# A state-space convolution in blocks of 1024: the sums of the second block's spectrum products move from VectorE and TensorE to accumulating transfers, under a new instruction order

## The chip, the cores and the metric

The kernel runs on one core of one Trainium2 chip. The metric is the device time in microseconds (us) of one execution. A profile of one execution is at hand for the kernel before; it names the engines PE (TensorE: matmuls), DVE (VectorE), ACT (ScalarE), POOL (GpSimd) and SP (SyncE, which here only issues transfers).

## The reference, cut to what matters

Two branches over 2048 tokens of 512 channels are mixed by a gate. Branch A is a long convolution, whose kernel K comes from a state-space model; branch B is a small expert network for the two tokens with the highest scores.

```python
P = jnp.exp(logdA[:, :, None] * l[None, None, :])
K = jnp.einsum("dn,dnl,dn->dl", Cc, P, dB).real        # 512 x 2048
...
Yf = Uf * Kf                                           # spectra, zero-padded to 2 L
y = irfft(Yf)[..., :L] + u * Dskip                     # branch A
...
r = x @ w_r; idx = argsort(-r)[:, :2]                  # branch B: two tokens
y = (silu(x_sel @ w_gate) * (x_sel @ w_up)) @ w_down
...
return g * a + (1 - g) * b
```

## The kernel before

**Blocks.** The sequence is cut into two blocks of 1024 tokens, and K likewise into K0 and K1. The spectra of the blocks are X0 and X1. The first block's result needs X0 K0. The second block's needs X1 K0 + X0 K1, and the sum of these two spectrum products is what the change is about. The 512 channels are handled in two halves (`h` = 0, 1) of 256, the frequencies in two quadrants (`qd` = 0, 1).

**Stages.** The order of the program text is this; engines run ahead of each other as far as the data allow.

1. Loads, exponentials and sines (`exps1`, `exps2`, `trig`, `tab1`, `tab2`) that give tables for K, mostly on ACT and DVE; the routing of branch B (`routing`) beside it.
2. `forward`: the spectra of the input by matmuls (L881).
3. `kgen(h)`: K at chosen lags by matmuls (L899), then a selection by matmuls (L912 to L928). Its last step multiplies an 8x256 result of these by a stored one on DVE.
4. `kspec(h)`: the spectrum of K by matmuls (L954), with a carry through the identity in the first half (L946).
5. `products(h, qds, blks)`: the spectrum products on DVE. For each half, block and quadrant, one 128x4096 product (all four combinations of real and imaginary parts) is written to a tile `p`; for the second block (`blk` 1) a second 128x4096 product, of X0 and K1, to a tile `t`. The two are summed, then real and imaginary parts combined (`u(0) - u(3)`, `u(1) + u(2)`: two of 128x1024), then written back to X as sums and differences of even and odd parts.
6. `inverse(h)`: ACT first copies a part of the output into PSUM (the seeds), then matmuls (L1028, and L1016 for a few edge tokens) add the inverse transform, ACT or DVE scales the result into the tile U (L1036), and 16 transfers of 128 KB write the output.

**How the second block is summed.** For three of the four pairs (half, quadrant) DVE adds the two tiles in one 128x4096 sum. For the pair named in `ACC`, (1, 0), PE adds them: identity matmuls (L990) form sum and combination in PSUM, and ACT moves the two results back.

**Order and places.** Nothing is scheduled at run time. `ORDER` is a string with the order of all operations, `SECOND` says which of two engines runs an operation that has a choice (evictions, scalings, squares: `EV`, `SCL`, `SQ` in the new kernel), `PLACES` which place in a pool of buffers a short-lived tile gets. `Prog` derives the semaphore waits from what each operation reads and writes. Each engine executes its own list strictly in order. A tile's place is free again when the last reader of its former tile has run. `late()` clears the edge tile OHR on POOL (L861), and SP's load of c_oh waits for it; the 2 MB load of the inverse matrices (c_inv, to tile G) and a part of the reload of U stand behind it in SP's queue.

Of the kernel before, what the change touches and what calls it, by code (L numbers as in the profile page):

```python
# [241 lines left out]
MUL1 = [(16, 4, 24, 4, 1), (20, 0, 24, 4, 1), (28, 15, 24, 4, -1)]  # L242
# [11 lines left out]
ACC = ((1, 0),)  # L254
# [98 lines left out]
def small_mats():  # L353
# [15 lines left out]
POOLS = {"pqa": 2, "pqb": 2, "pqc": 4}  # L369
ORDER = (  # L370
    "01l00200k01501600500000u00100400700o00p00q00601j01g00t00w00v01001201h01d01901e01100900r01a00300s01701x00801v00d00g00h02701t00x01r01y01400y01300c00f00z"
    "00l02500b00i01800a02801c01s01w01p01q00n00e02302601u02101z05n02402002201b03w04002901f06i01o01n03x08d03y06h08f05m02a02j03v02k01i04102l08e01m02b06j02m03z"
    "02n02c02o00m03702p05302q02r04202d02s06k02t06l04302u03404b05402v02w04506m04405h02x04802y04902z04a04c03003804603103204p04d05503904q04f03304704g04e04i04j"
    "03c03503l03d04h05g04k05o04m04r06p03g04l04n04u06q05q03h04o06n04s03i04w06o04t05604v06w03k00j03p03o06v06y06x03m03j06r08r01k06s04y03a04z03605p05707003n06z"
    "05805b05006t05i05907107204x07307405a08i08q05r05c06u07607505108g08j08h07807705205k08s05j05z07a03q08k07905d07h07b08t05l03b08u03r05e07c05s06003s07e07f03t"
    "07g07i08l06107j07d06606508n08v06306708x08o08y05f08m08w06206806909l06a08p08z07l07k07n09009206409u09m07m07o07q07z07r09107p09409309509n07s09o09r09609p07w"
    "07u09t07t07x09q09s09z0970980800a006b06c09c0990a20a102e09a09b09d08a06d09v09w05u05t09e0a30a408909g06f09h0a60a509x09f0a70a809i0aa06e0a905v07v05w07y05x03e"
    "06g08308403f09y09k0ac0ab08109j0ad0ae0820ag08b0af08508808c03u0aq0ar0ay0860aj0as0at05y0az0ao0ap0au0ah0ai0al0ak0am0an0b00b10av0aw0ax0ch0b80b90bc0be0870bb"
    "0bi0bf02f0ba0bd0bh0ci0cj0bg0bk0c40c10bj02g0ck0bz0cl0bl0bn0bm0b50bw02h0bo0b20b60c00b30b40br0c30bx0c20by0bp0bs0bq0bt0b70ct0bu02i0c50c60c70c90e80e70e90c8"
    "0cm0cu0bv0cn0co0cr0cv0d30cs0ea0cy0cb0eg0ez0cp0d40cw0cx0cz0eb0eh0cq0d10em0ep0d00e60d50ec0d20d60f40ed0e50d70f00f50ee0f10f20f60eq0df0er0ca0cc0dg0ei0es0f9"  # L380
    "0ef0f30ce0cd0f70f80dh0dn0fw0d80fx0dc0db0d90fy0ej0cf0dl0g40da0ek0en0et0fa0cg0dp0dv0dd0eu0di0dj0dk0do0dy0fz0de0eo0fs0g00dz0e00dq0dm0ds0g10g50dr0ft0fb0fc"
    "0g20fu0fv0el0fd0fe0fg0gc0gp0ff0dw0gm0dx0gd0g60g30go0gn0ge0gq0gt0gr0dt0fh0fi0fk0fj0ey0gf0g90gx0gu0ev0gg0ga0gs0e40e30du0gb0e20ew0e10g70gi0gw0gh0ex0gv0gz"
    "0fl0gk0fm0fo0fn0gl0gy0h80h00fp0h40fq0h10fr0h20g80gj0h50h30h60h70hh0hg0hc0h90ha0hd0he0hi0hf0hb0hj"
)
SECOND = (
    "000000000000000000000000000000000000100000000000000000000000000010101000101010100000000100000000000000000000000000100010000000000000000000000001000101"
    "001110010100010010000010010010000100000000000000000000000000000000000000000000000000000000001010000010000000000001000000000000000000000000000000000000"
    "000000000101000000010100011010000010011010000000100010001000001000000000000000000000000000000000000000000000000000000000000000000000000000000000000000"
    "000000000000000000000000000000000000000000000000000000000000000000000000000000000000000000000000000000000000000000000000000000000000001000000000000000"
    "00000000000000010000001100100000"  # L390
)
PLACES = (
    "2004756176414666666067000110100264042421011602064766100101111004004220204264646600000004406600706142350206200227354163"
# [4 lines left out]
def bass_gated_mix__ssm_conv_s4__moe_arch_mod__prompt_kernel(nc, A_u, A_A_re, A_A_im, A_B_re, A_B_im, A_C_re, A_C_im, A_log_dt, A_Dskip,  # L398
# [22 lines left out]
    with ExitStack() as es:  # L421
# [8 lines left out]
        def B(name, off, nbytes, dt=BF):  # L430
            assert off + nbytes <= SBW and off % 2 == 0, (name, off, nbytes)
            return Buf(P, name, AR, "sb", int(off), int(nbytes), dt)
# [9 lines left out]
        def nel(ap):  # L442
            r = 1
            for s, c in ap.ap[1:]:
                r *= c
            return r
# [3 lines left out]
        def TT(o, a, b, op, rd, wr, cst=None, **k):  # L450
            return P.op(DVE, lambda h: h.tensor_tensor(out=o, in0=a, in1=b, op=op), rd, wr, cost=cst or tt_cost(o, a, b), **k)  # L451
# [12 lines left out]
        def EV(o, a, rd, wr, **k):  # L464
            n = nel(o)
            return P.op((ACT, DVE), (lambda h: h.activation(out=o, in_=a, func=ACTF.Copy), lambda h: h.tensor_copy(o, a)), rd, wr,  # L466
                        cost=(0.185 + n * 0.833e-3, 0.16 + n * (1.04e-3 if a.dtype == F32 else 0.52e-3)), **k)
        def AFF(o, a, c, d, rd, wr):
            return P.op((DVE, ACT), (lambda h: h.tensor_scalar(out=o, in0=a, scalar1=c, scalar2=d, op0=ALU.mult, op1=ALU.add), lambda h: h.activation(out=o, in_=a, func=ACTF.Copy, scale=c, bias=d)), rd, wr, cost=(0.18, 0.2))
# [53 lines left out]
        PQR = [[B("pqa", oTI[0], 8 * KB), B("pqb", oTI[0] + 8 * KB, 8 * KB)], [B("pqc", oI, 16 * KB)] * 2]  # L523
        def place(pool, region, off, nbytes, dt=BF, n=1):
            def home(u):
                a = AR[:, (off + u * nbytes) // 2:(off + (u + 1) * nbytes) // 2]
                return (a if dt == BF else a.bitcast(dt)), 0
            return Life(P, pool, n, home, region, pool)
        OHR = B("ohr", oR, len(ERT) * 256)
        class Mem:  # L530
            def __init__(self, name):
                self.name, self.w, self.r, self.all, self.alias = name, {}, {}, [], []
# [80 lines left out]
        def pair(a, b):  # L613
            return bass.AP(a.tensor, a.offset, [a.ap[0], [b.offset - a.offset, 2]] + list(a.ap[1:]))
# [39 lines left out]
        def tab1(h, ts):  # L654
            tr = TP[h][1]
            e = lambda *ss: [(tr, ("e", s)) for s in ss]
            for o, a, b, n, d in MUL1:
                src = [a + i * d for i in range(n)]
                assert all(T1[o + i] == T1[x] + T1[b] for i, x in enumerate(src))
                v = lambda s0, st: tr(0, 128, 4 * s0, (128, 64), (st, n), (1, 4))  # L660
                TT(v(o, 4), v(a, 4 * d), v(b, 0), ALU.mult, e(b, *src), e(*range(o, o + n)))
# [32 lines left out]
        def tab2(h, ts):  # L694
# [11 lines left out]
            TT(pair(q2(0), q2(1)), pair(sq(eb, 0), sq(di, 0)), pair(sq(eb, 0), sq(di, 0)), MUL, ed, [(qa, 0), (qa, 1)])  # L706
# [254 lines left out]
        def products(h, qds, blks):  # L961
# [11 lines left out]
            tmp = lambda k: place("pq%s" % ("ab"[k] if h == 0 else "c"), PQR[h][k], (oTI[0] + 8 * k * KB, oI)[h], 8 * W, n=2)  # L973
            qk = lambda b, *ks: [(b, k) for k in ks]
            for blk in blks:
                p = tmp(0)
                TT(o2(p), x2(blk), k2(0), MUL, kx(blk) + kk(0, 0) + kk(0, 1), qk(p, 0, 1, 2, 3))
                if blk == 1:
                    t = tmp(1)
                    TT(o2(t), x2(0), k2(1), MUL, kx(0) + kk(1, 0) + kk(1, 1), qk(t, 0, 1, 2, 3))  # L980
# [14 lines left out]
                else:  # L995
                    if blk == 1:
                        TT(vall(p), vall(p), vall(t), ADD, qk(t, 0, 1, 2, 3), qk(p, 0, 1, 2, 3))
# [119 lines left out]
```

## Time and profile before

| What | Value |
|---|---|
| Median of 3 runs (lowest, highest) | 153.64 us (153.03, 154.14) |
| The profiled execution's own time | 153.67 us |
| Its span, first to last instruction | 151.9 us |
| Mean granted clock of TensorE | 0.988 |
| Busy: PE, DVE, ACT, POOL | 140.4, 140.1, 128.3, 6.7 us |
| 128x4096 products and sums on DVE | 15, mean 2282 ns |
| Identity matmuls that add the products (L990) | 16, 3.7 us busy |
| ACT's evictions of 128x1024 from PSUM | 34, mean 1021 ns |

A row of the groups has the line, the engine, the operation, what is written and read (partitions x elements), the count, then busy time and the mean of one in ns, then the idle time of the engine just ahead of them with what ended it. Many instructions of DVE have one line, 451, because a helper issues them; they are told apart by their shapes. In the chain of waits each row is a start, a length and the work that ran; "issue" is time in which an engine waited for nothing that the profile shows. In the slices, each digit stands for a fortieth of the span.

### The profile page before, as it was taken

How to read it: one execution, taken by the hardware profiler on the slowest of the kernel's cores; microseconds unless marked ns; L12 is line 12 of the kernel's file. 1: busy time of each engine (PE TensorE's matmuls, PEld its weight loads, DVE VectorE, ACT ScalarE, POOL GpSimd, SP SyncE). 2: the span in 40 equal slices, each digit the busy share in tenths (PEclk: the TensorE clock that was granted, in tenths of full speed). 3: DMA queues.
4: the chain of work that ended last, by engine and by line, in shares of the span. 5: the costliest groups of instructions: out<-in, count | busy, mean ns of one | idle time of the engine just before them, and what ended most of it. 6: DMA issues, size and time to landing. Idle time of an engine off the chain costs nothing.

```text
span 151.9 us, 3913 instructions
## 1 busy us (share of the span) xinstructions
PE 140.4 (92%) x1677; PEld 101.9 (67%) x1677; DVE 140.1 (92%) x201; ACT 128.3 (84%) x215; POOL 6.7 (4%) x13
## 2 busy tenths in 40 slices
PE   1977969999999999979999999999999999999990
PEld 1866633665446447975436889987888678888980
DVE  0489999999999999988999999999999999999972
ACT  3589999999999979998996568486999899899831
POOL 3000000000000000000540000010000000000000
PEclk9999999996899999999999999999999999999999
DMA  4899999939000001600029920007920000202166
GB/s 117 287 368 413 406 405 394 349 104 539 17 0 4 0 0 27 254 4 0 0 63 296 403 76 0 4 4 218 404 76 0 0 2 4 71 0 69 39 198 182
DMA packets 12435, 22.01 MB, mean 145 GB/s; under 512 B 1111, under 2 KB 8034, under 8 KB 12258
## 3 DMA queue, kind: packets, MB, share of 16 engines
q1 hardware_dynamic: 11410, 21.11, 39.4%
q10 hardware_dynamic: 976, 0.66, 1.5%
q8 instruction: 13, 0.21, 0.6%
q14 instruction: 4, 0.03, 0.1%
q0 software_dynamic: 32, 0.00, 0.1%
HBM read 19.66 MB, written 4.20 MB: 157 GB/s over the span
## 4 chain that ended last, share of the span: by engine, by line
PE 76%; DVE 13%; ACT 6%; issue 1%; DMA 1%; SPq 0%; DVEq 0%
PE ps L881 22%; PE ps L1028 18%; PE ps L954 12%; PE ps L899 8%; DVE AR L451 5%; ACT AR L466 3%; DVE AR L466 3%; PE ps L912 3%; PE ps L990 2%; PE ps L829 2%; PE ps L580 2%; ACT AR L462 2%; DMA AR<-c_bf 1%; PE ps L591 1%; DVE AR L472 1%
## 5 line engine op out<-in xcount | busy, mean ns | idle before, releaser
L451 DVE TENSOR_TENSOR AR<-AR 128x1024 bf16<-128x1024 bf16 (+8 forms) x132 | 118.5, 949 | 5.5 <-ACT AR L462 3.7
L466 ACT ACTIVATE AR<-ps 128x1024 bf16<-128x1024 f32 (+10 forms) x60 | 49.6, 861 | 11.3 <-PE ps L954 3.9
L881 PE MATMUL ps<-AR 128*128 128x512 bf16 x192 | 44.9, 389 | 0.0
L881 PEld LDWEIGHTS ps<-AR 128*128 128x128 bf16 x192 | 18.5, 100 | 21.8 <-issue 1.6
L1028 PE MATMUL ps<-AR 128*128 128x256 bf16 x256 | 29.3, 273 | 0.0
L1028 PEld LDWEIGHTS ps<-AR 128*128 128x128 bf16 x256 | 24.9, 98 | 3.5 <-DVE AR L451 0.3
L954 PE MATMUL ps<-AR 128*128 128x256 bf16 x160 | 19.0, 273 | 0.0
L899 PE MATMUL ps<-AR 128*128 128x84 bf16 (+1 forms) x512 | 18.0, 196 | 0.9 <-ACT AR L462 0.9
L899 PEld LDWEIGHTS ps<-AR 128*128 128x128 bf16 x512 | 17.9, 96 | 1.3 <-issue 1.0
L462 ACT ACTIVATE AR<-AR 128x1024 bf16<-128x1024 int16 (+5 forms) x24 | 18.2, 772 | 0.5 <-DVE AR L451 0.3
L462 ACT ACTIVATE ps<-AR 128x256 f32<-128x256 bf16 (+1 forms) x36 | 18.0, 545 | 0.1
L954 PEld LDWEIGHTS ps<-AR 128*128 128x128 bf16 x160 | 15.5, 98 | 2.9 <-DMA AR<-c_ksp 0.2
L1036 ACT ACTIVATE AR<-ps,AR 128x256 bf16<-128x256 f32 x27 | 11.8, 480 | 4.3 <-PE ps L1028 3.4
L472 ACT ACTIVATE AR<-AR 128x256 int32<-128x256 f32 (+3 forms) x30 | 14.7, 528 | 0.2 <-DVE AR L451 0.2
L462 ACT ACTIVATE AR<-ps 128x512 bf16<-128x512 f32 (+1 forms) x18 | 12.4, 773 | 2.3 <-PE ps L580 2.3
L650 ACT ACTIVATE AR<-AR 128x1024 int32<-128x1024 int32 (+1 forms) x9 | 8.2, 912 | 0.0
L472 DVE TENSOR_SCALAR AR<-AR 128x1024 bf16<-128x1024 bf16 (+3 forms) x20 | 7.3, 368 | 0.1
L591 PE MATMUL ps<-AR 128*128 128x128 bf16 x8 | 2.2, 488 | 3.4 <-DMA AR<-c_bf 3.4
L746 PE MATMUL ps<-AR 128*128 128x128 bf16 x64 | 4.3, 220 | 0.9 <-DVE AR L466 0.9
L580 PE MATMUL ps<-AR 128*128 128x128 bf16 x24 | 4.6, 414 | 0.2 <-DMA AR<-in_A_A_im_dram 0.2
L746 PEld LDWEIGHTS ps<-AR 128*128 128x128 bf16 x64 | 3.7, 99 | 1.3 <-DVE AR L466 1.1
L580 PEld LDWEIGHTS ps<-AR 128*128 128x128 bf16 x24 | 3.8, 183 | 1.0 <-DMA AR<-in_A_A_im_dram 0.5
(63 smaller groups left out, 81.7 us busy)
## 6 DMA issues: line engine op xcount, KB each, us to landing
AR<-c_ksp SPq DMA_DIRECT2D x5, 512.0 KB, 4.4
AR<-in_A_u_dram SPq DMA_DIRECT2D x4, 512.0 KB, 7.4
AR<-c_fwd SPq DMA_DIRECT2D x4, 512.0 KB, 8.8
AR<-out_dram SPq DMA_DIRECT2D x4, 512.0 KB, 7.0
AR<-c_inv SPq DMA_DIRECT2D x1, 2048.0 KB, 7.7
AR<-in_B_w_up_dram SPq DMA_DIRECT2D x1, 1792.0 KB, 13.3
AR<-in_B_w_gate_dram SPq DMA_DIRECT2D x1, 1792.0 KB, 18.1
out_dram<-AR SPq DMA_DIRECT2D x14, 128.0 KB, 2.2
```

The source lines that it names most:

```text
L451: return P.op(DVE, lambda h: h.tensor_tensor(out=o, in0=a, in1=b, op=op), rd, wr, cost=cst or tt_cost(o, a, b), **k)
L462: return P.op(ACT, lambda h: h.activation(out=o, in_=a, func=func, scale=scale, bias=bias), rd, wr, cost=0.185 + nel(o) * 0.833e-3 + (0.09 ...
L466: return P.op((ACT, DVE), (lambda h: h.activation(out=o, in_=a, func=ACTF.Copy), lambda h: h.tensor_copy(o, a)), rd, wr, cost=(0.185 + n * ...
L472: return P.op((ACT, DVE), (lambda h: h.activation(out=o, in_=a, func=ACTF.Copy, scale=c), lambda h: h.tensor_scalar(out=o, in0=a, scalar1= ...
L580: last = h.matmul(o, PRM(0, 128, i * D + k * 128, (1, 128)), DG(0, 128, k * 128, (1, 128)), start=(r + k == 0), stop=(r == reps - 1 and k ...
L650: P.op((DVE, ACT), (lambda hh: hh.tensor_scalar(out=w, in0=w, scalar1=16384.0, scalar2=None, op0=ALU.add), lambda hh: hh.activation(out=w, ...
L746: last = h.transpose(bb(0, 128, db * 256 + t_ * 128, (1, 128)), U(0, 128, (2 * q + t_) * D + db * 128, (1, 128)), IDN(0, (1, 128)))
L881: last = h.matmul(o, w, x, start=(pm + par + st == 0), stop=(par == 1 and st == 3), skip_group_check=(pm == 1))
L899: last = hh.matmul(pb(0, 128, g // 6 * 512 + g % 6 * W4 + o, (1, n)), TP[h][1 - i // 2](0, 128, (b0 + g) * 128, (1, 128)), r[i](0, 128, (b ...
L954: last = hh.matmul(pb(0, 128, n * 256, (1, 256)), KP[u](0, 128, tau * 128, (1, 128)), KC[h](0, 128, jg * 256, (1, 256)), start=(k == 0 and ...
L1028: r = hh.matmul(pb(0, 128, e * 256, (1, 256)), G(0, 128, ((par * 2 + part) * 4 + ft) * 512 + (2 * t2 + e) * 128, (1, 128)), X(0, 128, h * ...
L1036: P.op((ACT, DVE), (lambda hh, o=o, i_=i_, g_=g_: hh.activation(out=o, in_=i_, func=ACTF.Copy, scale=g_), lambda hh, o=o, i_=i_, g_=g_: hh ...
```

## The change

- For all four pairs in `DAC` the two tiles of the second block are summed by a transfer that POOL issues: it reads `t` and adds it to `p`, SBUF to SBUF, 1 MB each (two runs of 2048 elements per partition). `ACC` is empty, so PE and ACT no longer take part; the combination of the pair (1, 0) is DVE's now, as for the others.
- The product tiles get four places instead of three regions: `a`, `b` (the first quadrant of the first half and the second quadrant of the second half), `c` (the other two pairs, two places) and `d` (block 0).
- `SQ` gives some squares a choice of engine, and one table entry of `MUL1` is made by squaring instead of by a product.
- `ORDER`, `SECOND` and `PLACES` are new throughout. What the prediction refers to: in SP's queue the load of log_dt stands third instead of first; on POOL the first two accumulating transfers stand ahead of the clearing of OHR, the other two behind it; on DVE block 0's products of the first half stand between the first two transfers' issues and their readers.

```diff
-MUL1 = [(16, 4, 24, 4, 1), (20, 0, 24, 4, 1), (28, 15, 24, 4, -1)]
+MUL1 = [(16, 4, 24, 4, 1), (20, 0, 24, 4, 1), (28, 7, None, 4, -1)]
...
-ACC = ((1, 0),)
+ACC = ()
+DAC = ((0, 0), (0, 1), (1, 0), (1, 1))
...
-POOLS = {"pqa": 2, "pqb": 2, "pqc": 4}
+POOLS = {"pqa": 1, "pqb": 1, "pqc": 2, "pqd": 2}
...
+        def SQ(o, a, rd, wr):
+            n = nel(o)
+            return P.op((DVE, ACT), (lambda h: h.tensor_tensor(out=o, in0=a, in1=a, op=ALU.mult), lambda h: h.activation(out=o, in_=a, func=ACTF.Square)), rd, wr,
+                        cost=(0.157 + n * 0.52e-3, 0.185 + n * 0.833e-3))
...
-        PQR = [[B("pqa", oTI[0], 8 * KB), B("pqb", oTI[0] + 8 * KB, 8 * KB)], [B("pqc", oI, 16 * KB)] * 2]
+        PQO = {"a": (oTI[0],), "b": (oTI[0] + 8 * KB,), "c": (oI, oI + 8 * KB), "d": (oR + 24 * KB, oTI[1])}
+        PQR = {k: Both(*[B("pq%s%d" % (k, i), o, 8 * KB) for i, o in enumerate(os_)]) for k, os_ in PQO.items()}
+        def pq(h, blk, qd, k):
+            key = "d" if blk == 0 else ("ab"[k] if h == qd else "c")
...
             for blk in blks:
-                p = tmp(0)
+                p = pq(h, blk, qds[0], 0)
...
                 if blk == 1:
-                    t = tmp(1)
+                    t = pq(h, blk, qds[0], 1)
...
                     if blk == 1:
-                        TT(vall(p), vall(p), vall(t), ADD, qk(t, 0, 1, 2, 3), qk(p, 0, 1, 2, 3))
+                        if (h, qds[0]) in DAC:
+                            v = lambda b: b(0, 128, 0, (2048, 2), (1, 2048))
+                            P.op(POOL, lambda hh, p=p, t=t: hh.dma_start(v(p), v(t), accum_op=ADD, max_dma_last_dim=4096), qk(t, 0, 1, 2, 3), qk(p, 0, 1, 2, 3), cost=1.3, nbytes=1048576, dma=True, tag="acc")
+                        else:
+                            TT(vall(p), vall(p), vall(t), ADD, qk(t, 0, 1, 2, 3), qk(p, 0, 1, 2, 3))
                     TT(u(0), u(0), u(3), SUB, qk(p, 3), qk(p, 0))
                     TT(u(1), u(1), u(2), ADD, qk(p, 2), qk(p, 1))
```

## The prediction

> **What bounds the kernel now.** I read the first part of the page (busy time), then the chain of waits in order of time, then the timeline of VectorE (DVE) over the last third, then the groups with shapes kept apart, then the transfers.
>
> ```profile
> span 151.9 us, 3913 instructions
> PE 140.4 (92%) x1677; PEld 101.9 (67%) x1677; DVE 140.1 (92%) x201; ACT 128.3 (84%) x215; POOL 6.7 (4%) x13
> ```
>
> Two engines are nearly full, TensorE (PE) and DVE. The averages don't say which sets the end; the chain does. Its columns are start, length, and what ran:
>
> ```profile
> 66.31 2.62 PE ps L899 x72
> ...
> 118.61 0.44 PE ps L954 x4
> 119.05 1.73 PE ps L990 x8
> 120.77 0.11 PE ps L1016
> 120.88 1.73 PE ps L990 x8
> 122.61 2.62 PE ps L1028 x24
> ...
> 142.91 4.82 PE ps L1028 x44
> 147.73 0.03 issue
> ```
>
> From 66.31 to 147.73 us PE is the chain, with almost no gap. The identity matmuls that add products today (L990) lie in it with 2 x 1.73 us. But DVE is no looser, as its timeline shows (start, length, group):
>
> ```profile
> 99.70 9.55 DVE L451 TENSOR_TENSOR AR<-AR 128x4096 bf16<-128x4096 bf16 x8
> 109.28 0.42 DVE L451 TENSOR_TENSOR AR<-ps,AR 8x256 bf16<-8x256 f32 x1
> 109.73 36.23 DVE L451 TENSOR_TENSOR AR<-AR 128x1024 bf16<-128x1024 bf16 x34
> ```
>
> So taking work from one of the two gains nothing; it must come from both, and the order must keep both fed. The change does take from both.
>
> **Part by part, with the prices.** Shapes and means:
>
> ```profile
> L451 DVE TENSOR_TENSOR AR<-AR 128x4096 bf16<-128x4096 bf16 x15 | 34.0, 2282 | 0.1
> L466 ACT ACTIVATE AR<-ps 128x1024 bf16<-128x1024 f32 x34 | 33.6, 1021 | 5.4 <-PE ps L954 3.9 <-PE ps L881 0.9 <-PE ps L990 0.6
> L451 DVE TENSOR_TENSOR AR<-AR 128x1024 bf16<-128x1024 bf16 x50 | 32.4, 683 | 1.5 <-PE ps L899 1.2
> ```
>
> *PE.* 16 matmuls of L990 go: 2 x 1.73 = 3.5 us of the chain.
>
> *DVE.* Three sums of 128x4096 go: 3 x 2.28 = 6.8 us. The fourth sum was PE's and included the real and imaginary combination, so DVE gets that combination back: two of 128x1024, 2 x 0.68 = 1.4 us. The instruction order shows seven small ones more on DVE than before (scalings, two evictions, one output scaling), about 2.1 us by their rows. Net 6.8 - 1.4 - 2.1 = 3.3 us less, by rows that overlap their neighbours by 0.08 us.
>
> *ScalarE (ACT).* Two evictions (2 x 1.02 us) and seven small ones less; ACT has idle time before its evictions in the same rows, so I count nothing. The squares written as SQ stay DVE products of the same shape: nothing.
>
> *Start.* The load of log_dt goes from first to third in SP's queue. SP issues every 0.45 us there, so it comes 0.9 us later; PE waits for another load until 3.39 us anyway, and DVE's first product (3.69 us) is fed by it through ACT. I count +0.6 us.
>
> *New waits.* In the new order the second half's products for block 0 stand behind DVE's 8x256 product, which reads a late PE result (the selection matmuls). Laying the new order out with these durations (an instruction starts when its engine is free and its inputs are done; PE at 0.216 us per 512 columns), DVE waits there for 2 us, and PE waits 3 to 4 us in pieces for ACT's evictions and PSUM seeds between 99 and 115 us. In the old order PE has no wait there; part of these pieces only uses up time by which PE is earlier by then. I count +1.6 us on the way to the end. Bounds: 0 (the waits vanish in an earlier PE) and 3.5 (all of the gain on PE).
>
> *Sum without the transfers:* -3.5 + 0.6 + 1.6 = -1.3 us. The gain is small because the two shortened engines now wait for each other.
>
> *The four accumulating transfers.* Each moves 1 MB from one tile onto another; no row of before shows one. The nearest rows:
>
> ```profile
> AR<-c_ksp SPq DMA_DIRECT2D x5, 512.0 KB, 4.4
> AR<-c_inv SPq DMA_DIRECT2D x1, 2048.0 KB, 7.7
> out_dram<-AR SPq DMA_DIRECT2D x14, 128.0 KB, 2.2
> out_dram<-AR POOLq DMA_INDIRECT x1, 5.8
> L854 POOL DMA_INDIRECT out_dram<-AR x1 | 3.8, 3806 | 0.2 <-issue 0.2
> ```
>
> From 128 KB (2.2 us) to 2048 KB (7.7 us) a transfer costs 2.9 us more per MB. A plain 1 MB would land after 2.2 + 0.875 x 2.9 = 4.7 us. An addition needs the source and the old target read: 2 MB, as c_inv, 7.7 us. If the write takes its own turn, 3 MB: 10.6 us. Issue: SP's take 0.4 us, POOL's one issue 3.8 us, of which some is reading its index list. Bounds of the whole: 4.7 and 10.6 + 3.4 = 14 us. I take two reads and 1 us of POOL, 7.7 + 0.6 = 8.3 us.
>
> The Trainium skill, Collectives: The Full Stack, section "The bandwidth ceiling", says that an add in the transfer engines costs no arithmetic time but a second source read on the same reading side, halving the rate. By it the 8.3 us stand; by its DMA: Bandwidth & Descriptors, section "Anatomy of one DMA", a 1 MB transfer would take 2.0 + 1.05 MB / 436 GB/s = 4.4 us, an estimate for a plain copy. No run here shows an add of this size yet.
>
> What hides them is the DVE work that the new order puts between a transfer's issue (after its second 128x4096 product) and its first reader, a 128x1024 combination:
> - first (first half, quadrant 0): two products, an eviction and small ones, 6.2 us, and 2.5 us of waits: 8.7 us
> - second (first half, quadrant 1): the waits again, the first one's combinations, two products: 10.4 us
> - third (second half, quadrant 0): three products, four 128x1024 and some halves: 10.2 us
> - fourth (second half, quadrant 1): one product, five 128x1024, five halves, two scalings: 7.8 us, and 0.4 us until PE runs dry: 8.2 us
>
> With 8.3 us all four just fit. Beyond that each pair stalls DVE separately (DVE executes in order, so everything behind the combination waits, and PE's inverse matmuls with it): a common landing time of 9, 10 or 12 us costs 1.2, 3.2 or 7.2 us.
>
> *POOL's queue.* The clearing of the edge tile (L861 before) now stands behind the first two transfers, and SP's c_oh, c_inv and reload wait for it. Before, it ran at 101.6 us and c_inv landed at 110.2, 1.8 us ahead of the first inverse matmul (112.0). The second transfer is issued at about 99 us, so even 3.8 us on POOL cost 1.1 us, under that cover; without the cover they would be 1.1 us on PE.
>
> **Forecast.** All four land in time: 153.7 (the profiled execution: span 151.9 and 1.8 around it) - 1.3 = 152.4 us. Its median of three is 153.64, the same. Own range 151.2 to 153.6. Chance 0.42.
>
> **Rivals.**
>
> *Second transfer late.* c_inv and the reload behind it (2.5 MB) start at about 102.5 us, just when the second transfer's reading (5.2 us at c_inv's rate) begins. If both share evenly, 4.4 us of it become 8.8, it lands at 112.2 instead of 109.3, and DVE stalls 2.9 us: 155.3; half of that 153.9. For: c_inv's window in the old trace shows the engines full (0.85 busy, 340 GB/s in 104 to 108 us). Against: no two queues are seen competing there. Chance 0.22, half of it slower by over 1%.
>
> *The addition is slow.* Three passes or 3 us of POOL per issue: 10.6 to 12 us and more, and both pairs stall. Place: the combinations behind transfers one and four; price 2 us per us beyond 8.2; it decides from 9.0 us on. At 12 us 152.4 + 7.2 = 159.6. For: POOL's only issue in the trace took 3.8 us, and no row shows an add at full rate. Against: that issue reads indices, this one moves long rows. Chance 0.24, slower.
>
> *DVE locks POOL out.* POOL writes this transfer's descriptors while DVE runs. If a DVE instruction holds POOL until it ends, each issue waits up to one 128x4096 product, 2.3 us: 8.3 becomes 10.6, 152.4 + 2 x 2.3 = 157.0. For: DVE has no gap to give. Against: the instructions there are nearly all TENSOR_TENSOR, which run slower than the scalings of the same size (0.683 against 0.415 us for 128x1024) and need not hold what those hold. Chance 0.05.
> This is a rule of the Trainium skill, SBUF — State Buffer, section "Who interferes with whom": DVE's two-port modes keep POOL from writing descriptors, and it exempts two-input products. If the exemption holds, the rival falls.
>
> *More than forecast.* The new waits come to nothing: -3.5 + 0.6 = -2.9, 150.8 us. For: the old order shows both engines full without them. Against: my layout of the order. Chance 0.07.
>
> **How the numbers follow.** A measurement here tells about 1% from no change (1.5 us). The forecast's 0.42 splits at 152.1 into 0.18 faster and 0.24 the same; with the last rival (0.07) faster is 0.25. The second transfer's case gives 0.11 the same and 0.11 slower, the other two slower cases 0.29, of which 0.01 the same: same 0.36, slower 0.39. The range runs from 150.8 to 159.6, the slow case at 12 us; above it lies about 0.1, below it 0.04.
>
> **What would show it.** Issue to landing of POOL's four transfers: 8.3 us, the second up to 13. DVE idle ahead of a 128x1024 combination, released by a DMA: none if the forecast holds; over 1 us twice means the slow addition, once (before the third transfer) the sharing. L990 gone and PE waiting for ACT between 99 and 115 us for 3 to 4 us. DVE's busy time near 137 us. The prediction is wrong if a wait for POOL's transfers shows in the chain, or if the end moves with no such wait.

## The result, and the profile after

| Kernel | Median | Lowest to highest | Ratio to before (95% interval) |
|---|---|---|---|
| before | 153.64 us | 153.03 to 154.14 | 1 |
| changed | 155.69 us | 155.34 to 155.79 | 1.0131 (1.0091 to 1.0171) |

The change makes the kernel about 1.3% slower; the forecast was 152.4 us, 0.8% faster. All ratios below leave out runs that were disturbed on the chip, so a median over all runs need not give the ratio beside it.

The head of the page of the changed kernel, whose profiled execution took 155.34 us:

```profile
span 153.5 us, 3887 instructions
PE 138.1 (90%) x1661; PEld 100.0 (65%) x1661; DVE 137.3 (89%) x207; ACT 124.4 (81%) x206; POOL 9.7 (6%) x17
```

PE is 2.3 us less busy than before and DVE 2.8, and the span is 1.6 us longer: both engines stand still more. The chain of waits shows where it goes through (start, length, what ran):

```profile
81.92 10.50 DVE AR L452 x10
...
97.54 10.16 DMA AR<-AR
107.70 0.02 issue
107.72 11.17 DVE AR L452 x14
...
123.37 14.11 DVE AR L452 x10
...
138.71 10.83 PE ps L1052 x96
```

Before, PE was this chain from 66 us on. Now it is DVE, then the first accumulating transfer, then DVE again up to 138.7 us, and only then PE's last inverse matmuls. The timeline of DVE has the wait in its last column:

```profile
105.48 0.42 DVE L452 TENSOR_TENSOR AR<-ps,AR 8x256 bf16<-8x256 f32 x1 [1.28 <-PE ps L937]
107.72 35.07 DVE L452 TENSOR_TENSOR AR<-AR 128x1024 bf16<-128x1024 bf16 x38 [1.82 <-DMA AR<-AR]
```

The four transfers, each from the transfer view in a window around its issue (the last number is the time from issue to landing, in us), in order, and c_inv behind them:

```profile
AR<-AR POOLq DMA_DIRECT2D x1, 1024.0 KB, 10.2
...
AR<-AR POOLq DMA_DIRECT2D x1, 1024.0 KB, 11.6
...
AR<-AR POOLq DMA_DIRECT2D x1, 1024.0 KB, 7.9
...
AR<-AR POOLq DMA_DIRECT2D x1, 1024.0 KB, 8.2
...
AR<-c_inv SPq DMA_DIRECT2D x1, 2048.0 KB, 14.6
```

The second half's two land as forecast (8.3 us); the first half's don't. The first was issued at 97.54 and DVE was ready for it at 105.90: a cover of 8.4 us for 10.2. And c_inv, 7.7 us before, now takes 14.6 and makes PE wait for the first inverse matmul. PE's timeline between 102 and 120 us:

```profile
102.65 0.66 PE L946 MATMUL ps<-AR 128*32 128x64 bf16 x16 [0.64 <-DVE AR L467]
...
107.13 3.67 PE L975 MATMUL ps<-AR 128*128 128x256 bf16 x32 [0.71 <-ACT AR L467]
111.23 2.36 PE L975 MATMUL ps<-AR 128*128 128x256 bf16 x20 [0.43 <-ACT ps L463]
114.64 0.68 PE L1040 MATMUL ps<-AR 128*128 128x256 bf16 x2 [1.05 <-ACT ps L463]
...
119.30 0.92 PE L1052 MATMUL ps<-AR 128*128 128x256 bf16 x7 [1.40 <-DMA AR<-c_inv]
```

Four of these five waits name no transfer (0.64, 0.71, 0.43 and 1.05 us). The experiments must tell the price of the new order alone from that of its transfers; kspinvshort below, where no transfer is late, has the same four.

### The profile page after: what moved, and what is told of

It reads as the page before. It is cut to its first block, busy times and chain, and to the rows that moved or that the text cites. A ratio compares the mean times of both kernels' runs of the same rounds, so it can differ in the third digit from the quotient of the medians.

```text
span 153.5 us, 3887 instructions
## 1 busy us (share of the span) xinstructions
PE 138.1 (90%) x1661; PEld 100.0 (65%) x1661; DVE 137.3 (89%) x207; ACT 124.4 (81%) x206; POOL 9.7 (6%) x17
## 3 DMA queue, kind: packets, MB, share of 16 engines
q0 software_dynamic: 1120, 4.20, 15.6%
## 4 chain that ended last, share of the span: by engine, by line
DVE 47%; PE 36%; DMA 9%; ACT 3%; issue 3%; SPq 1%
DVE AR L452 39%; PE ps L902 18%; PE ps L1052 7%; DMA AR<-AR 7%; PE ps L920 6%; DVE AR L467 3%; PE ps L850 2%; DMA AR<-in_A_log_dt_dram 2%; DVE AR L477 2%; ACT AR L463 1%; PE ps L598 1%; DVE AR L456 1%; DVE AR L459 1%; PE ps L864 1%; DVE AR L797 1%
## 5 line engine op out<-in xcount | busy, mean ns | idle before, releaser
L452 DVE TENSOR_TENSOR AR<-AR 128x1024 bf16<-128x1024 bf16 (+10 forms) x127 | 110.6, 923 | 7.8 <-ACT AR L463 5.4
L467 ACT ACTIVATE AR<-ps 128x1024 bf16<-128x1024 f32 (+10 forms) x57 | 48.2, 865 | 14.1 <-PE ps L975 4.7
L902 PEld LDWEIGHTS ps<-AR 128*128 128x128 bf16 x192 | 18.8, 101 | 21.4 <-issue 1.9
L1052 PEld LDWEIGHTS ps<-AR 128*128 128x128 bf16 x256 | 24.7, 98 | 5.5 <-DVE AR L452 2.7
L975 PE MATMUL ps<-AR 128*128 128x256 bf16 x160 | 19.3, 273 | 1.5 <-ACT AR L467 0.7
L975 PEld LDWEIGHTS ps<-AR 128*128 128x128 bf16 x160 | 15.3, 98 | 5.4 <-ACT AR L467 1.8
L920 PEld LDWEIGHTS ps<-AR 128*128 128x128 bf16 x512 | 17.9, 96 | 0.7 <-ACT AR L696 0.4
L477 ACT ACTIVATE AR<-AR 128x256 int32<-128x256 f32 (+2 forms) x25 | 12.4, 528 | 0.0
L668 ACT ACTIVATE AR<-AR 128x1024 int32<-128x1024 int32 (+1 forms) x10 | 8.9, 888 | 0.1
L1019 POOL DMA_DIRECT2D AR<-AR x4 | 4.9, 1216 | 60.4 <-DVE AR L452 30.6
L477 DVE TENSOR_SCALAR AR<-AR 128x256 int32<-128x256 f32 (+3 forms) x25 | 8.4, 350 | 0.0
L767 PE MATMUL ps<-AR 128*128 128x128 bf16 x64 | 4.4, 220 | 1.8 <-DVE AR L452 1.2
L767 PEld LDWEIGHTS ps<-AR 128*128 128x128 bf16 x64 | 3.6, 98 | 2.6 <-DVE AR L452 1.4
L933 PE MATMUL ps<-AR 128*32 128x128 bf16 x64 | 4.7, 421 | 0.6 <-ACT AR L467 0.6
L609 PE MATMUL ps<-AR 128*128 128x128 bf16 x8 | 2.0, 475 | 3.1 <-DMA AR<-in_A_C_im_dram 3.1
## 6 DMA issues: line engine op xcount, KB each, us to landing
AR<-c_fwd SPq DMA_DIRECT2D x4, 512.0 KB, 10.2
AR<-c_inv SPq DMA_DIRECT2D x1, 2048.0 KB, 14.6
AR<-in_B_w_up_dram SPq DMA_DIRECT2D x1, 1792.0 KB, 11.6
```

Source lines behind the costliest of these rows:

```text
L668: P.op((DVE, ACT), (lambda hh: hh.tensor_scalar(out=w, in0=w, scalar1=16384.0, scalar2=None, op0=ALU.add), lambda hh: hh.activation(out=w, ...
L767: last = h.transpose(bb(0, 128, db * 256 + t_ * 128, (1, 128)), U(0, 128, (2 * q + t_) * D + db * 128, (1, 128)), IDN(0, (1, 128)))
L902: last = h.matmul(o, w, x, start=(pm + par + st == 0), stop=(par == 1 and st == 3), skip_group_check=(pm == 1))
L920: last = hh.matmul(pb(0, 128, g // 6 * 512 + g % 6 * W4 + o, (1, n)), TP[h][1 - i // 2](0, 128, (b0 + g) * 128, (1, 128)), r[i](0, 128, (b ...
L975: last = hh.matmul(pb(0, 128, n * 256, (1, 256)), KP[u](0, 128, tau * 128, (1, 128)), KC[h](0, 128, jg * 256, (1, 256)), start=(k == 0 and ...
L1019: P.op(POOL, lambda hh, p=p, t=t: hh.dma_start(v(p), v(t), accum_op=ADD, max_dma_last_dim=4096), qk(t, 0, 1, 2, 3), qk(p, 0, 1, 2, 3), cos ...
```

## The experiments

`moved(ORDER, a, b)` in the diffs takes operation a out of the order and puts it in ahead of b. The line of DVE's helper is 452 to 472 in these kernels, depending on the lines added.

**Less to move.** First the transfers themselves: a sum over 1/32 of the elements (short), and a plain copy in place of the sum (plain).

```diff
-v = lambda b: b(0, 128, 0, (2048, 2), (1, 2048))
+v = lambda b: b(0, 128, 0, (2048, 2), (1, 64))          # short
...
-hh.dma_start(v(p), v(t), accum_op=ADD, max_dma_last_dim=4096)
+hh.dma_start(v(p), v(t), max_dma_last_dim=4096)         # plain
```

> Each accumulating transfer adds only 64 of the 2048 elements of a run (1/32 of the sum; the rest of the addition is left out), at the same places in the order. It shows what the new order takes when its transfers cost almost nothing. Theory A (the loss is made by the transfers: the first one lands 1.8 us late on DVE and c_inv, slowed from 7.7 to 14.6 us, holds PE for 1.4 us): both waits go, c_inv is back under 9 us, and the time falls from 155.7 by about 2 us to 153.3 to 153.9. Theory B (the new order is slow in itself: the later start, and DVE and PE waiting for ACT): the time stays at 155 or more, with the two waits gone but others in their place.

> The four transfers copy the tile instead of adding it (the sum of the second block's two products is left out). Same bytes written, one read fewer. If an addition is slow because of its second read: a packet of 4096 bytes takes about half of the 0.35 us that it takes in the changed kernel, the lone third transfer lands 5 us after its issue instead of 7.9, and the time is near that of the short transfers (153.3 to 154.2). If copies between two places of SBUF are slow whatever they do: packets of 0.35 us, 7.9 us, and 155.5 us as in the changed kernel.

Measured: short 154.89 us, ratio 1.0093 (1.0062 to 1.0124); plain 155.07, 1.0063 (1.0023 to 1.0103). DVE has no wait for a transfer in either, and c_inv is back to 8.6 us in short, yet little of the loss comes back. The queue lines of the page (packets, MB, share of 16 engines' span) of the changed kernel and then of plain show what an addition costs the transfer engines:

```profile
q0 software_dynamic: 1120, 4.20, 15.6%
```

```profile
q0 software_dynamic: 1120, 4.20, 7.4%
```

The same packets, twice the time: 0.34 us each when adding, 0.16 when copying (15.6% of 16 x 153.5 us over 1120 packets, and 7.4% of 16 x 153.4). The third transfer lands after 4.6 us as a copy and 7.9 us as a sum.

Why so little came back is in PE's timeline of short, at the first matmul of `kspec` (L975):

```profile
84.19 1.47 PE L975 MATMUL ps<-AR 128*128 128x256 bf16 x12 [1.76 <-ACT AR L467]
```

In the changed kernel's profile that wait is 0.23 us. In short it is 1.76, and everything up to the first 128x1024 combination is 1.6 us later, about what the missing wait for the transfer gave. ACT is named, but it had finished by then; of that below.

**Keeping c_inv out of the way.** If the sharing of the engines is the loss, the order of SP's queue should matter. early puts the two reloads of U ahead of a third, earlywait also lets c_inv wait for the first transfer, defer puts c_inv ahead of one reload.

```diff
+ORDER = moved(ORDER, "0c0", "0bz")   # early, earlywait: reload 432 ahead of 431
+ORDER = moved(ORDER, "0by", "0bz")   # early, earlywait: reload 430 ahead of 431
...
+P.ops[434].deps.add(P.ops[-1].idx)   # earlywait: c_inv waits for the first sum
...
+ORDER = moved(ORDER, "0c2", "0c0")   # defer alone: c_inv ahead of reload 432
```

> In SP's queue two 512 KB reloads of U move from beside c_inv to the group of reloads ahead (77 to 80 us), where the transfer engines are free. Theory A (sharing): 1 MB less runs between 104 and 120 us; c_inv lands 2 to 3 us earlier (about 117 instead of 119.2), PE's wait for it (1.4 us) goes, and the first accumulating transfer's last part lands earlier than 107.7; time 154.5 to 155.2. Theory B: 155.5 to 155.8, no change, since the end hangs on DVE.

> As the kernel with the two reloads moved, and c_inv is issued only when the first accumulating transfer has landed. Theory A: nothing of SP's shares the engines with the first transfer, which lands about 8 us after its issue (105.5 instead of 107.7), so DVE's wait of 1.8 us is gone or under 0.4; c_inv is issued near 105.6 and lands by 116, without a wait of PE; time 153.6 to 154.3. Theory B: the wait goes but the time stays within 0.4 us of 155.7. If instead the second accumulating transfer, behind the first on the same queue, is what slows the first one's last part, the first still lands at 107 and the wait stays.

> The 2 MB load of c_inv goes ahead of the 0.5 MB reload of U behind which it stands in SP's queue; nothing else is changed. Theory A (VectorE's wait for the first transfer, 1.8 us at 107.7, sets the end through VectorE's products up to 138.6): c_inv lands about 1.3 us earlier, near 117.9, TensorE's wait for it (1.56 us at 119.30) shrinks to about 0.3, and the end moves by no more than 0.3 us, since TensorE waits for VectorE at 138.7 anyway: 155.3 to 155.7. Rival B (c_inv, held back by the transfers, sets the end): the end moves by the full 1.3 us, to 154.4. Rival C (c_inv takes the engines from the second transfer, as when the reloads were moved): the second transfer lands 1 us or more after 113.6, VectorE waits again, 156 to 157.

Measured: early 159.87 us, 1.0331 (1.0293 to 1.0369); earlywait 157.55, 1.0279 (1.0251 to 1.0307); defer 160.81, 1.0359 (1.0296 to 1.0422). Each is worse than the changed kernel. The reload between the transfers and c_inv was a shield: without it c_inv meets the second transfer head on. In the changed kernel it is the reload that runs beside the second sum. The queues (q0 has the sum) from 106 to 111 us:

```profile
q0 software_dynamic: 194, 0.79, 83.7%
q1 hardware_dynamic: 193, 0.37, 22.5%
```

In earlywait it is c_inv. The sum is nearly through when c_inv's packets begin; from 111 to 112 us both run:

```profile
q1 hardware_dynamic: 15, 0.25, 59.1%
q0 software_dynamic: 17, 0.06, 57.6%
```

Each time there are as many packets of the one as of the other, whatever their size. The reload's have about 2 KB to the sum's 4 (0.37 MB / 193, 0.79 MB / 194), so the sum gets twice the bytes; c_inv's have 16 KB (0.25 MB / 15), so c_inv gets four times the sum's. The second sum took 13.1 us in earlywait (11.6 in the changed kernel), and DVE waited:

```profile
115.35 3.10 DVE L461 TENSOR_TENSOR AR<-AR 128x1024 bf16<-128x1024 bf16 x5 [2.34 <-DMA AR<-AR]
```

The Trainium skill, DMA: Bandwidth & Descriptors, section "Queues, rings and completion order", says that each engine changes between its queues only at packet borders, in turn. The equal counts above agree with turns; a packet of that page holds several descriptors, and no view here tells whether a packet of the profile is one.

**One late thing at a time.** split issues each sum as two halves, the half that is read first in front; splitdefer adds defer's move; dtfirst puts log_dt back to the front; inv loads 1/32 of c_inv.

```diff
+for part in ((0, 1) if h == qds[0] else (1, 0)):        # split, splitdefer
+    v = lambda b, part=part: b(0, 128, 1024 * part, (3072 - 2048 * part, 2), (1, 1024))
+    ks = ((0, 3), (1, 2))[part]
+    ... hh.dma_start(v(p), v(t), accum_op=ADD, ...), qk(t, *ks), qk(p, *ks) ...
...
+ORDER = moved(ORDER, "002", "000")                      # dtfirst
...
-DMA([(G(0, 128, 0, (1, 8192)), g_c[:, :])], [], [G], 2097152)
+DMA([(G(0, 128, 0, (1, 256)), g_c[:, 0:256])], [], [G], 2097152)   # inv
```

> Each 1 MB accumulating transfer is issued as two of 0.5 MB, the half first whose combination VectorE runs first; the order is otherwise the same. Theory A: the first half of the first transfer lands near 103.5, 4 us before VectorE asks for it, the second about 107 to 108; VectorE's wait of 1.8 us is gone, VectorE's products run 1.5 to 1.8 us earlier, but TensorE's first inverse matmul still waits for c_inv near 119.2 and has only 0.5 us of wait after that: 155.0 to 155.4 with TensorE's wait for c_inv grown to about 3 us. Rival B (the order itself, TensorE's waits for ScalarE between 111 and 115 us): the wait for the transfer goes and comes back as a wait elsewhere on VectorE, the end moves by less than 0.2 us, 155.5. Rival D (twice the issues cost POOL and the transfer engines more than they save): a half takes over 6 us, 156 to 157.

> Both edits together: each accumulating transfer in two halves, and c_inv ahead of the U reload in SP's queue. Theory A: both waits of the window from 99 to 120 us shrink (the first transfer's by 1.8 us, c_inv's end by 1.3 us), so the end moves by the smaller of the two, 1.2 to 1.8 us: 153.9 to 154.5. Rival B (the new order's own waits): less than 0.4 us, 155.3. Under the summed need of the engines (2 x 5.2 us for the transfers and 7.7 us for c_inv from 99.4 us on) c_inv can't land before 117.5, so below 153.7 would say that the engines carried more than their rows show.

> The load of log_dt goes back to first place in SP's queue, everything else as in the changed kernel. The first VectorE product comes 1.2 us earlier (near 3.7 instead of 4.85). If the head's delay reaches the end in full: 154.5. If it is taken up on the way (TensorE's routing at 17.4 us begins at the same time in both kernels, at 27 us 0.6 us remain): 0 to 0.6 us, 155.1 to 155.7; theory A expects 155.3.

> The load of the inverse matrices brings 256 of its 8192 columns (1/32; the rest of G keeps what was there), the four transfers add in full. Theory A (several things are late in the same window because they share the transfer engines, and each hides behind the next): the second transfer lands 2 to 3 us earlier than 113.6, TensorE's wait for c_inv (1.56 us) is gone, but the first transfer's last piece and VectorE's chain behind it (107.7 to 138.6) stay: 154.9 to 155.5. Rival B (the lateness of c_inv sets the end): 1.5 us less, 153.8. Rival C (the new order itself): 155.3 with the same time lost as waits for ScalarE and TensorE.

Measured: split 156.35 us, 1.0143 (1.0091 to 1.0195); splitdefer 156.41, 1.0108 (1.0051 to 1.0166); dtfirst 157.01, 1.0182 (1.0134 to 1.0230); inv 155.74, 1.0118 (1.0073 to 1.0162). None differs clearly from the changed kernel, though each took away what it was meant to. In split the first half landed after 5.1 us and DVE had no wait; in inv PE had no wait for c_inv. But in inv the second sum still took 11.4 us (103.09 to 114.51), so theory A's "2 to 3 us earlier" was wrong: it isn't c_inv that holds it up there but the first sum, half of it still to come when the second is issued 4.5 us behind it in the same queue, and the reload. splitdefer's profiled execution (span 152.2 us) had no stretch of lowered clock (mean granted 1.000 against 0.989); it is no proof of a gain.

What these runs have in common shows in their timelines side by side: how long PE waited at the first matmul of `kspec`, what DVE waited for, and when DVE began the first 128x1024 combination.

| Profiled run | PE's wait at `kspec` | DVE's wait for a sum | First combination |
|---|---|---|---|
| changed | 0.23 us | 1.82 us, first | 107.72 us |
| short | 1.76 | none | 107.60 |
| plain | 2.04 | none | 107.70 |
| split | 1.53 | none | 107.35 |
| inv | 2.15 | 0.69, second | 107.54 |
| dtfirst | 0.81 | 0.71, second | 106.93 |

Two late things hold the same place, and in each of these profiles at least one of them is there. The wait at `kspec` comes some 15 us ahead of the first sum's issue, so no edit to the sums can have made it: how long it is differs from run to run.

**VectorE adds one pair.** In dac3 DVE makes the second sum itself, in its idle time behind an eviction; dac3dt has log_dt in front as well.

```diff
-DAC = ((0, 0), (0, 1), (1, 0), (1, 1))
+DAC = ((0, 0), (1, 0), (1, 1))
+ORDER = moved(ORDER, "0cc", "02e")
+ORDER = moved(ORDER, "002", "000")   # dac3dt alone
```

> VectorE adds the second pair (first half, quadrant 1) itself, in one 128x4096 sum of 2.28 us put behind its eviction for the selection matmuls; the other three pairs keep their transfers. Theory A: VectorE stands still for 1.4 + 1.9 us just there (ahead of 105.5 and of 107.7), the sum fills that, one transfer less stands against c_inv, which lands 3 us earlier; VectorE's products run about 1 us earlier: 154.0 to 154.6. Rival (VectorE is the bound and its idle time isn't where the sum is put): 2.28 us more, 157.6.

> As the run before, and log_dt is loaded first in SP's queue again, so that VectorE's first product comes 1.2 us earlier. With nothing of the second transfer to wait for, what the head gives should pass through: 0.4 to 0.8 us less than the run before, 153.4 to 154.0, about the time of the kernel before the change. If the head is taken up elsewhere: the same as the run before.

Measured: dac3 157.03 us, 1.0200 (1.0147 to 1.0253); dac3dt 156.43, 1.0188 (1.0133 to 1.0242). c_inv landed at 113.95 us (119.17 in the changed kernel), earlier still than expected, and it was of no use: the sum stood ahead of small products that PE waits for (1.55 us ahead of the selection matmul at 106.20), so the selection matmuls and the 8x256 product behind them came 2.3 us later (107.80). Idle time on DVE that a chain of other engines causes is not free time.

**Both sums and c_inv, and c_ksp.** invshort makes the four transfers and c_inv small. ksp makes the loads of c_ksp small, which `kspec` reads (five, not the four that the expectation names); short_first makes only the first half's two transfers small; ksp_first does both of these; kspinvshort makes c_ksp, c_inv and all transfers small.

```diff
-DMA([(KP[u](0, 128, 0, (1, 2048)), kp_c[:, u * 2048:(u + 1) * 2048])], [], [KP[u]], 524288)
+DMA([(KP[u](0, 128, 0, (1, 128)), kp_c[:, u * 2048:u * 2048 + 128])], [], [KP[u]], 524288)   # ksp
...
-v = lambda b: b(0, 128, 0, (2048, 2), (1, 2048))
+v = lambda b: b(0, 128, 0, (2048, 2), (1, 64 if h == 0 else 2048))                         # short_first
```

> Both are made small: c_inv brings 1/32 of its columns and each of the four transfers adds 64 of every 2048 elements. What is left is the new order with nothing late in that window. If the layout of the prediction was right but for the transfers, 152.4 or less. If the order's own waits (TensorE for c_ksp near 84 us and for ScalarE between 111 and 117, VectorE for TensorE at 105) eat what the shorter engines gain, 153.3 to 154.5, no better than before. I expect 153.6.

> The four loads of c_ksp bring 128 of 2048 columns each (the rest keeps what was there), all else as in the changed kernel. Theory A (late things hide behind each other): TensorE's wait at 82 to 84 us falls below 0.4 us and the first transfer is issued up to 1.5 us earlier than in a run with a late c_ksp, but both transfers and c_inv still share the engines, and the second can't land before about 112.5; 154.8 to 155.5. Rival E (the wait for c_ksp is what the new order loses): 153.6 to 154.2, the time of before.

> Only the first half's two transfers are small (64 of every 2048 elements), the second half's two add in full, c_inv and c_ksp are full. Theory A: the second half's transfers land in time (8 us after their issue, as predicted) and cost nothing: the same as with all four small, 154.5 to 155.2. Rival F (the second half's transfers, which stand against the output's, cost as much as the first's): 155.3 or more.

> c_ksp brings 1/16 of its columns and the first half's two transfers are small; c_inv and the second half's transfers are full. Theory A: the waits for c_ksp, for the two transfers and for c_inv are gone (c_inv lands near 112), only the order's own remain: 152.7 to 153.3. Rival E (c_ksp alone is the cost): the same as with c_ksp small alone. Rival F (the second half's transfers cost): over 154.

> c_ksp brings 1/16 of its columns, c_inv 1/32, and each of the four transfers adds 64 of every 2048 elements: nothing of the new order is late through a transfer. If the shorter engines are worth the 1.3 us that the prediction counted, 152.0 to 152.6 in the median and little spread. If the order's own waits between TensorE, ScalarE and VectorE (about 3.5 us on TensorE between 99 and 118 us) eat it, 153.3 to 153.9. I expect 152.7.

| Run | Small | Median | Ratio to before |
|---|---|---|---|
| changed | nothing | 155.69 us | 1.0131 (1.0091 to 1.0171) |
| short | all sums | 154.89 | 1.0093 (1.0062 to 1.0124) |
| ksp | c_ksp | 155.25 | 1.0083 (1.0029 to 1.0137) |
| short_first | first half's sums | 155.77 | 1.0106 (1.0045 to 1.0167) |
| ksp_first | c_ksp, first half's sums | 153.29 | 0.9934 (0.9894 to 0.9974) |
| invshort | c_inv, all sums | 154.09 | 1.0011 (0.9974 to 1.0049) |
| kspinvshort | c_ksp, c_inv, all sums | 153.14 | 0.9943 (0.9900 to 0.9985) |

Either cut alone gives back less than half a per cent, both together 2.0% (1.0131 to 0.9934). Part of this goes with the clock that each execution was granted, but not all: at 0.986 to 0.989 the four executions of ksp took 154.59 to 155.23 us, the four of ksp_first 153.37 to 154.50. That settles what the loss through transfers is made of: the first half's two sums, and c_ksp, in parallel. With both gone, nothing is left for the second half's sums and the full c_inv: ksp_first has them, and is no slower than kspinvshort.

One row doesn't fit so simply. invshort differs from short by c_inv alone and has c_ksp in full, yet its ratio is 0.8% lower. Its twelve executions spread from 152.69 to 156.95 us, and PE's wait at `kspec` is 0.80 us in its profile and 1.76 in short's; c_inv is issued 20 us behind that wait and can't have shortened it. Whether c_inv costs something while c_ksp is late stays open.

ksp_first's transfers (the two sums of the second half, then c_inv):

```profile
AR<-AR POOLq DMA_DIRECT2D x2, 1024.0 KB, 8.0
...
AR<-c_inv SPq DMA_DIRECT2D x1, 2048.0 KB, 8.3
```

short_first shows c_ksp's part at its largest, in the wait of PE's first `kspec` matmul:

```profile
83.94 1.82 PE L975 MATMUL ps<-AR 128*128 128x256 bf16 x13 [2.38 <-ACT AR L467]
```

The name is misleading: ACT's last eviction for it ended at 81.42 us and c_ksp landed at 83.85. Of that load's 16 pieces 15 had landed by 82.31 us; in plain 15 had by 82.97, and the last came at 84.43. It is one late piece each time, and why it is late was not tested. With c_ksp small PE starts within 0.1 us of the eviction's end (82.12 after 82.05 in ksp).

**The same cuts in the kernel before.**

> The kernel before, with c_ksp's loads bringing 128 of 2048 columns each. Its trace shows TensorE without a wait for c_ksp, so the theory that lateness of c_ksp is a cost of the new order expects no change: 153.2 to 153.9, ratio within 0.3% of 1. The rival (the old order waits for it too in most runs) expects 152.5, and then the new order is worth nothing even with everything in time.

> The kernel before with c_ksp (1/16 of its columns) and c_inv (1/32) both small. c_inv lands 1.8 us ahead of its first reader in the old order, so nothing more should come of it: the same as with c_ksp small alone, 153.2 to 153.9. The difference between this run and the new order with the same small loads (0.993 to 0.994) is what the new order with hidden transfers is worth, about 0.9 us, against 1.3 in the prediction.

Measured: before_ksp 152.27 us, 0.9953 (0.9921 to 0.9986); before_kspinv 152.73, 0.9972 (0.9942 to 1.0003). The expectation of no change within 0.3% was wrong for c_ksp: the old order too loses some of its time to this load, though before_kspinv's interval reaches 1. What is gone in the profiles of both is not a wait at `kspec` but a stop of PE of 0.93 us in `kgen`, ahead of the matmuls at 66.31 us and 7 us behind the issue of c_ksp's first two loads. In before a 16 KB packet of instruction loading runs between 64 and 65 us, when these two loads are through; in the two others one runs between 60 and 63. That the stop is for instructions held back by c_ksp was not tested. So the 0.9943 of kspinvshort isn't a gain of the new order. With the same loads small, new order and old are 0.9943 and 0.9972, with intervals that overlap: no difference that these runs can tell.

## Why the prediction was wrong

**What bounds it, and the work that goes.** Right. The 16 matmuls of L990 are gone; DVE's busy time is 137.3 us ("near 137"). PE's busy time fell by 2.3 us and not by 3.5, because it is 1.3 us busier in the first 27 us, where it stood still as much less.

**Start, +0.6 us.** The first DVE product came 1.2 us later (4.86 us), but PE's routing started at 17.40 us, as before (17.46). dtfirst gained nothing: its chain of waits has the same three DVE products at 29.07 us, the changed kernel's at 29.04. This term should have been about 0.

**New waits, +1.6 us: the first step that failed.** The layout said that PE would wait 3 to 4 us between 99 and 115 us, and half of that was taken to use up time by which PE is earlier. It came as laid out, and in the sum it counts in full: the term was put at half its size. The windows from 99 to 118 us (length, then busy time of PE, PEld, DVE, ACT and POOL, the clock, the transfers' share and rate) of before, of the changed kernel, and of kspinvshort, where no transfer is late:

```profile
99.00:118.00 19.00, 18.97 (x248) 15.76 (x245) 18.84 (x19) 16.64 (x24) 0.52 (x1) 1.00 0.38 140
```

```profile
99.00:118.00 19.00, 15.83 (x223) 12.60 (x219) 15.59 (x22) 14.23 (x23) 1.75 (x2) 1.00 1.02 262
```

```profile
99.00:118.00 19.00, 15.93 (x219) 12.59 (x216) 17.56 (x25) 14.12 (x22) 1.75 (x2) 1.00 0.27 64
```

PE stands still 0.03 us in the first, 3.17 in the second, and 3.07 in the third. With 3.1 for this term and 0 for the start the sum is 153.7 - 3.5 + 3.1 = 153.3 us without transfers; kspinvshort's profiled execution took 153.44 at the same granted clock as the changed kernel's (0.989). So the removed matmuls are paid back within 20 us as PE's waits for DVE, ACT and the selection's round trip, and the new order is worth nothing measurable even with all transfers hidden.

That is bookkeeping on PE, and not a test of each wait. The chain of kspinvshort from 102 us on has PE at the selection (to 105.38 us) and at the end, and DVE in between:

```profile
105.38 0.42 DVE AR L452
...
105.83 11.18 DVE AR L452 x14
...
136.82 10.73 PE ps L1052 x96
```

PE's waits for ACT between 107 and 117 us aren't on this path; DVE's wait for the selection (1.28 us ahead of 105.38, where the layout had 2) is. PE, too, stands still for only 0.14 us from 118 to 137 us, so both engines lead to about this end, and no run tells which of their waits would have to go.

**Transfers, 8.3 us against covers of 8.7, 10.4, 10.2 and 8.2: the second step that failed, for one half.** The price was right for a sum with little beside it, the second half's: 7.9 and 8.2 us, the second of them landing at 143.75 us for a reader at 143.78. An addition halves the rate (0.34 against 0.16 us a packet), and POOL's issue took 1.2 us where 1 was assumed:

```profile
L1019 POOL DMA_DIRECT2D AR<-AR x4 | 4.9, 1216 | 60.4 <-DVE AR L452 30.6
```

By the Trainium skill, Collectives: The Full Stack, section "The bandwidth ceiling", an add costs a second source read and with it half the rate; the time of a packet agrees, the second read itself no view shows. The mistake was to treat the four as independent. The first half's two are issued 4.5 us apart, and each occupies the engines for about 6 us (1120 / 4 packets of 0.34 us on 16 engines), so the second stands behind the first, and c_oh, the reload and c_inv share what is left. That accounts for the second sum, 11.6 us here and 11.4 in inv, where DVE waits for it. The second half's are issued 5.6 us apart, with only 128 KB outputs beside them, and just fit, by 0.03 us. In the changed kernel's profile the first sum itself cost 1.9 us: with everything small DVE's combinations start at 105.83 us, here at 107.72, and PE's last stretch at 138.71 us in place of 136.82.

```profile
105.83 35.08 DVE L452 TENSOR_TENSOR AR<-AR 128x1024 bf16<-128x1024 bf16 x38
```

Of its 16 pieces 15 had landed by 105.60, ahead of the reader and 8.1 us after the issue, as priced; the last landed at 107.70. So this wait is one late piece, like c_ksp's, and the sharing of the two sums isn't shown to be its reason. At 105.7 us a 16 KB packet of instruction loading took 0.96 us of one engine; that it was that engine, and that it is the reason, was not tested.

Two figures beside this were off. The second transfer was put at about 99 us and issued at 102.00; by 8.3 us it would have landed alone at 107.3, and the 109.3 that the prediction sets against 112.2 is its reader's time (99 + 10.4). And c_inv, behind POOL's clearing of OHR, was issued 2.0 us later than before (104.55 after 102.51), where 1.1 was counted.

**c_ksp: not in the prediction.** The new order brings PE to `kspec` at 82.1 to 82.6 us, where the old one began it at 83.88, and c_ksp lands differently from run to run: at 82.52 us in the profile of the changed kernel, 83.85 in short_first's, 84.43 in plain's. In the profile of before load and reader met within 0.05 us (83.83 and 83.88), with 0.2 us of wait for c_ksp on PE's weight loads and none on its matmuls. A wait of nearly zero with no slack behind it was read as no risk.

**The rivals.** "Second transfer late" named the sharing with c_inv and the reload. The place was wrong (the first sum's tail made DVE wait, the second's only when the first was out of the way), but sharing there was. "The addition is slow" falls: 7.9 us where little else runs. "DVE locks POOL out" falls: four issues of 1.2 us beside a busy DVE. The Trainium skill, SBUF — State Buffer, section "Who interferes with whom", exempts two-input products from that lock, and this agrees. "More than forecast" (the waits come to nothing) falls with the waits.

**What stays open.** How c_ksp's lateness and the first sums' add up in one execution is read from profiles of single executions; that they run in parallel is shown by the four ratios of ksp, short_first, ksp_first and the changed kernel. Why one piece of a load or a sum lands 0.5 to 2.1 us behind the other 15 is open too. None of these runs shows a version faster than both kernels: the best that hiding every transfer gives is the time of the old order.

## What to carry to other kernels

When work is taken from two full engines, the gain is what is left after the new order's own waits, and a wait that a layout of the order shows counts in full unless the profile names the later slack that absorbs it. Transfers on one set of engines are one resource: add up the engine time of everything issued in the window (here two sums, a reload and c_inv between 99 and 120 us) before giving each its time alone. A load that lands just as its reader starts is a wait of nearly zero in the profile and the next wait as soon as anything ahead of the reader gets faster; and when taking away one late thing changes nothing, take away two.

## What the runs showed of the hardware

- Two transfers of different packet size on two queues share the engines by packets, not by bytes: 193 packets of about 2 KB against 194 of 4 KB in 5 us of the changed kernel, 15 of 16 KB against 17 of at most 4 KB in 1 us of earlywait.
- A 1 MB accumulating transfer within SBUF takes 7.9 to 8.2 us from issue to landing with nothing but 128 KB outputs beside it, a copy of the same shape 4.5 to 4.6.
- The last of a transfer's 16 pieces can come late and set its landing: 83.85 us against 82.31 for the other 15 of a 512 KB load (short_first), 107.70 against 105.60 for those of a 1 MB sum (changed kernel).
